# Another order for the steps of an attention and mixer kernel, from the first token mixing on

## The chip, the core and the metric

The kernel runs on one core of a Trainium2 chip. The metric is device time in microseconds (us): the median of the runs. The engines are TensorE (PE; its weight loads are listed as PEld), VectorE (DVE), ScalarE (ACT), GpSimd (POOL) and SyncE (SP, which here only starts DMAs).

## The reference

Two stages, all in float32. The first is delta-rule attention over 4 batches, 8 heads, 768 positions and 48 columns a head; the second mixes tokens at rank 32 and then channels.

```python
k_n = k / (norm(k) + 1e-06)
for t in range(S):                                   # S = 768
    y[:, :, t] = einsum('bhd,bhde->bhe', q[:, :, t], state)
    v_old = einsum('bhde,bhd->bhe', state, k_n[:, :, t])
    state = state + beta[t] * outer(k_n[:, :, t], v[:, :, t] - v_old)

x = y with its heads side by side                    # (4, 768, 384)
u = x + (x.transpose(0, 2, 1) @ U @ V).transpose(0, 2, 1)    # U 768x32, V 32x768
out = u + maximum(u @ w_ch1, 0) @ w_ch2              # 384 -> 1536 -> 384
```

## The kernel before, in words

**The attention.** The 768 positions of a batch are cut into 12 chunks of 64, and a batch into two units of 6 chunks: units n0 to n7 for batches b0 to b3. For each unit, `grams` turns k and q (`turn`, PE at L672, or for n3 on `turn_blocks`, transposes on DVE at L747) and multiplies them (`products`, L700; i0 is k with k, i1 is k with q; their results leave by ACT at L720 or DVE at L731). A triangular system per chunk is then inverted: `blocks` (L771) does so for blocks of 32 on DVE, one pair of instructions (prod at L803, xt at L809) per column, after a transpose (gs, L794) and before another (zz, L816); `joins` (L838), once for each half h0 and h1 of a unit, joins the blocks by small matmuls of 32*32 (L860 and L874 for n2 alone, with an ACT copy at L865 and a DVE step at L878 between them; then L900 and L903, an ACT copy at L908, then L918 and L921); `diagonals` (L933) puts the blocks in place by four ACT copies (L939) and two POOL memsets (L946). `prepare` (L1014; matmuls L1023 and L1034) applies the inverse to k and v. `recur` (L955) walks a batch's 12 chunks one after another, by matmuls of 16 small pieces at L1072 and L1100 with DVE steps between (z at L1085, s at L1111); `outputs` (L975; L983 and L997) forms a chunk's result, and ACT at L967 puts it into X.

**The mixer.** A batch has three groups of 256 positions, i0 to i2. `front` (L1381) multiplies X by U once a batch (L1393, with a DVE copy tt), by V for each group (L1412), adds on DVE, and turns the sum (L1436) into ut by an ACT copy (L1439). `wide` (L1449) holds the channel mixing of a group: `channels` e0 to e5 (L1465; two steps each of 6 matmuls at L1497), each followed by `relu` on ACT (L1462); `add_up` on DVE (L1524); `narrow` e0 to e3 (L1574; seven steps in a group, each 12 matmuls of L1617 in the trace), each step followed by `gather` on DVE (L1537), which adds into X and lets the result be stored. The second product of the mixing is written with seven products in place of eight, which needs the sums S1 and S2 and the weight sums. The last batch takes its first product by seven products too: `quick` (L1283), six times (f0 to f5), with matmuls at L1296, ACT copies and a final relu.

**Weights.** `load_weights` (L1147) brings fp32 weights in as pieces (`start`, SP's DMAs), which ACT (`raised`, L1198) and DVE (L1211, L1219, L1226) put into the form that PE multiplies.

**What sets the order.** Each of these functions is a generator: it yields `op(engine, cost, ...)` (L101) ahead of every step it issues and `need(...)` (L114) where it depends on a key that another announces by `emitted` (L117). `ORDER` (L144 to L350) is a table from the step's place, 0 to 2258, to the name of the generator that makes its next step there. `run()` (L381) goes through the table and advances that generator, so the instructions of every engine, and the DMAs of the SP and POOL queues, are issued in the order of the table; each engine works its own queue in order, and waits on semaphores where data or a buffer is missing. The costs in `op` play no part in what is issued. `free["pair"]` holds the four pairs of PSUM banks: a step with `take="pair"` gets the one that came free first by the table's order, and a step with `give` puts it back; `reserve` (L1442) takes pair 3 out for the mixer (its two banks are "mix"). `QUADRANTS` (L351) is empty, so full matmuls keep the form 128*128 ("F" in the code); the steps of `products`, `prepare`, `recur`, `outputs` and L1412 use 64*64 or the like ("Q"), `joins` 32*32 ("J"), L1393 128*32 ("T").

Of the kernel before, what the change touches and what calls it, by code (L numbers as in the profile page):

```python
# [27 lines left out]
def kernel(  # L28
# [116 lines left out]
    add_up b0 i0 f00: 573 585 613; add_up b0 i0 f03: 645 676 690; add_up b0 i1 f00: 795 797 800; add_up b0 i1 f03:  # L145
    818 819 824; add_up b0 i2 f00: 942 944 1042; add_up b0 i2 f03: 1023 1051 1071; add_up b1 i0 f00: 1161 1166 1186;
    add_up b1 i0 f03: 1189 1190 1191; add_up b1 i1 f00: 1309 1337 1363; add_up b1 i1 f03: 1357 1359 1368; add_up b1
    i2 f00: 1488 1493 1571; add_up b1 i2 f03: 1564 1572 1576; add_up b2 i0 f00: 1695 1717 1737; add_up b2 i0 f03:
    1728 1729 1730; add_up b2 i1 f00: 1888 1895 1906; add_up b2 i1 f03: 1886 1889 1901; add_up b2 i2 f00: 1992 2000
    2026; add_up b2 i2 f03: 2046 2047 2049; add_up b3 i0 f00: 2185 2186 2188; add_up b3 i0 f03: 2191 2192 2195;  # L150
    add_up b3 i1 f00: 2201 2202 2207; add_up b3 i1 f03: 2208 2209 2210; add_up b3 i2 f00: 2227 2228 2236; add_up b3
    i2 f03: 2224 2225 2229; blocks n0: 61 73 75 76 82 84 86 88 89 91 93 94 96 97 103 110 114 122; blocks n1: 143 157
    160 163 173 175 179 192 201 206 208 212 213 215 218 219 226 229; blocks n2: 479 496 501 502 508 512 513 514 515
    516 518 519 525 532 534 536 539 542; blocks n3: 704 720 721 729 730 733 739 741 761 765 769 771 772 773 778 779
    780 781 783 785 786 787 791 798 801 802 813 815 823 828 829 834 836 838; blocks n4: 971 982 985 987 989 996 1007
    1009 1012 1036 1038 1039 1040 1064 1074 1077 1082 1083 1087 1090 1107 1116 1119 1120 1122 1127 1129 1131 1132
    1133 1137 1138 1139 1140; blocks n5: 1168 1195 1198 1207 1218 1225 1227 1230 1231 1236 1241 1244 1249 1259 1269
    1271 1276 1278 1281 1286 1288 1291 1293 1294 1298 1311 1313 1314 1316 1323 1324 1332 1333 1351; blocks n6: 1510
    1523 1532 1541 1547 1558 1563 1566 1567 1568 1569 1596 1603 1612 1616 1617 1620 1622 1624 1645 1649 1653 1660
    1663 1665 1666 1671 1672 1673 1674 1675 1681 1684 1699; blocks n7: 1713 1724 1725 1739 1741 1744 1757 1762 1767  # L160
    1773 1775 1780 1782 1783 1800 1806 1807 1810 1817 1824 1829 1834 1837 1838 1849 1850 1856 1857 1860 1865 1866
    1867 1879 1881; both f0: 2149; both f1: 2105; both f2: 2147; both f3: 2123; both f4: 2111; both f5: 2184;
    channels b0 i0 e0: 546 547; channels b0 i0 e1: 549 550; channels b0 i0 e2: 552 553; channels b0 i0 e3: 567 574;
    channels b0 i0 e4: 588 591; channels b0 i0 e5: 604 633; channels b0 i1 e0: 768 776; channels b0 i1 e1: 777 788;
    channels b0 i1 e2: 790 792; channels b0 i1 e3: 799 803; channels b0 i1 e4: 806 807; channels b0 i1 e5: 808 814;
    channels b0 i2 e0: 898 899; channels b0 i2 e1: 907 912; channels b0 i2 e2: 935 936; channels b0 i2 e3: 950 959;
    channels b0 i2 e4: 965 969; channels b0 i2 e5: 995 1005; channels b1 i0 e0: 1118 1130; channels b1 i0 e1: 1136
    1148; channels b1 i0 e2: 1150 1151; channels b1 i0 e3: 1153 1155; channels b1 i0 e4: 1156 1158; channels b1 i0
    e5: 1159 1175; channels b1 i1 e0: 1297 1299; channels b1 i1 e1: 1300 1302; channels b1 i1 e2: 1304 1305; channels
    b1 i1 e3: 1306 1307; channels b1 i1 e4: 1326 1327; channels b1 i1 e5: 1342 1343; channels b1 i2 e0: 1430 1431;  # L170
    channels b1 i2 e1: 1432 1449; channels b1 i2 e2: 1450 1469; channels b1 i2 e3: 1470 1497; channels b1 i2 e4: 1498
    1501; channels b1 i2 e5: 1516 1530; channels b2 i0 e0: 1650 1654; channels b2 i0 e1: 1656 1669; channels b2 i0
    e2: 1686 1687; channels b2 i0 e3: 1689 1692; channels b2 i0 e4: 1697 1698; channels b2 i0 e5: 1700 1701; channels
    b2 i1 e0: 1808 1812; channels b2 i1 e1: 1813 1831; channels b2 i1 e2: 1833 1841; channels b2 i1 e3: 1843 1869;
    channels b2 i1 e4: 1871 1873; channels b2 i1 e5: 1874 1876; channels b2 i2 e0: 1950 1959; channels b2 i2 e1: 1960
    1961; channels b2 i2 e2: 1973 1979; channels b2 i2 e3: 1987 1999; channels b2 i2 e4: 2011 2027; channels b2 i2
    e5: 2033 2037; copies f0: 2127 2136; copies f1: 2082 2095; copies f2: 2129 2142; copies f3: 2086 2107; copies f4:
    2085 2103; copies f5: 2166 2168; cut f0 k0 to0: 2173; cut f0 k0 to1: 2169; cut f0 k1 to1: 2152; cut f1 k0 to0:
    2139; cut f1 k0 to1: 2106; cut f1 k1 to1: 2112; cut f2 k0 to0: 2153; cut f2 k0 to1: 2158; cut f2 k1 to1: 2163;
    cut f3 k0 to0: 2146; cut f3 k0 to1: 2154; cut f3 k1 to1: 2206; cut f4 k0 to0: 2171; cut f4 k0 to1: 2137; cut f4  # L180
    k1 to1: 2165; cut f5 k0 to0: 2181; cut f5 k0 to1: 2187; cut f5 k1 to1: 2194; diagonals n0 h0: 188 190 191 195 210
    222; diagonals n0 h1: 167 169 171 176 181 186; diagonals n1 h0: 312 315 319 336 343 353; diagonals n1 h1: 290 292
    303 338 349 358; diagonals n2 h0: 576 577 578 579 595 600; diagonals n2 h1: 632 646 665 670 705 707; diagonals n3
    h0: 854 855 860 865 870 873; diagonals n3 h1: 848 849 885 905 960 966; diagonals n4 h0: 1160 1162 1172 1197 1200
    1215; diagonals n4 h1: 1164 1192 1205 1211 1223 1226; diagonals n5 h0: 1356 1361 1365 1375 1402 1413; diagonals
    n5 h1: 1354 1380 1392 1419 1443 1444; diagonals n6 h0: 1708 1710 1711 1738 1745 1749; diagonals n6 h1: 1712 1723
    1726 1747 1753 1754; diagonals n7 h0: 1899 1905 1913 1931 1942 1945; diagonals n7 h1: 1892 1898 1911 1912 1918
    1957; first f0: 2160; first f1: 2097; first f2: 2135; first f3: 2138; first f4: 2092; first f5: 2180; front b0
    i0: 495 500 506 509 524 537; front b0 i1: 556 562 602 624; front b0 i2: 634 640 672 680; front b1 i0: 1055 1065
    1066 1078 1091 1111; front b1 i1: 1216 1224 1232 1237; front b1 i2: 1338 1348 1412 1425; front b2 i0: 1595 1599  # L190
    1605 1608 1623 1628; front b2 i1: 1633 1661 1702 1764; front b2 i2: 1801 1811 1835 1845; front b3 i0: 2041 2042
    2048 2050 2052 2054; front b3 i1: 2055 2061 2062 2067; front b3 i2: 2068 2070 2074 2076; gather b0 i0 h0 c0
    finalFalse: 671; gather b0 i0 h0 c0 finalTrue: 695; gather b0 i0 h0 c1 finalTrue: 756 1010; gather b0 i0 h1 c0
    finalFalse: 710; gather b0 i0 h1 c0 finalTrue: 757 805; gather b0 i0 h1 c1 finalFalse: 715; gather b0 i0 h1 c1
    finalTrue: 738; gather b0 i1 h0 c0 finalFalse: 820; gather b0 i1 h0 c0 finalTrue: 831; gather b0 i1 h0 c1
    finalTrue: 896 1061; gather b0 i1 h1 c0 finalFalse: 851; gather b0 i1 h1 c0 finalTrue: 881 1367; gather b0 i1 h1
    c1 finalFalse: 868; gather b0 i1 h1 c1 finalTrue: 867; gather b0 i2 h0 c0 finalFalse: 1017; gather b0 i2 h0 c0
    finalTrue: 1041; gather b0 i2 h0 c1 finalTrue: 1105 1185; gather b0 i2 h1 c0 finalFalse: 1079; gather b0 i2 h1 c0
    finalTrue: 1097 1163; gather b0 i2 h1 c1 finalFalse: 1084; gather b0 i2 h1 c1 finalTrue: 1086; gather b1 i0 h0 c0
    finalFalse: 1188; gather b1 i0 h0 c0 finalTrue: 1204; gather b1 i0 h0 c1 finalTrue: 1272 1778; gather b1 i0 h1 c0  # L200
    finalFalse: 1229; gather b1 i0 h1 c0 finalTrue: 1277 1591; gather b1 i0 h1 c1 finalFalse: 1238; gather b1 i0 h1
    c1 finalTrue: 1247; gather b1 i1 h0 c0 finalFalse: 1358; gather b1 i1 h0 c0 finalTrue: 1378; gather b1 i1 h0 c1
# [1080 lines left out]
    def quick(f):  # L1283
# [77 lines left out]
        mm(px, w1_of(f + HF, 1), t4)  # L1361
        mm(px, w1_of(f + HF, 2), t5, stop=True)
        emitted(("quick", f))
        yield op("act", act(384), rush=True)
        nc.scalar.activation(c(1, 0), px, ACTF.Relu)
        emitted(("cut", 1, 0, f), 0.06)
        yield need(("out", f))
# [328 lines left out]
```

## Time and profile before

| what | value |
|---|---|
| time, median of 3 runs | 599.98 us |
| the three runs | 596.76, 601.71, 599.98 us |
| profiled execution, span from first to last instruction | 594.9 us |
| profiled execution, own time | not given; the median stands 5.1 us above the span |
| mean granted TensorE clock | 0.943 |
| instructions in the trace | 23426 |
| DMA, read and written in HBM | 29.98 MB and 4.72 MB |
| PE, costliest lines | L1497 150.1 us (x648); L1617 w_sb,hs 96.7 us (x540) |
| DVE, costliest lines | L809 64.6 us, L803 63.3 us (x200 each) |
| ACT, costliest lines | L939 32.4 us (x64), L1462 32.2 us (x54) |

How to read it: the share of an engine's busy time is over the whole span; a matmul's end is modelled, so the start of the next step is the surer mark. "Idle before" is time in which an engine stood still just ahead of an instruction, followed by the releaser, the work that ended last ahead of it. The chain follows what released what, back from the last instruction. Position 500 of the table lies at about 110.6 us: the L1393 step of `front b0 i0`, at position 495, begins at 108.55.

### The profile page before, as it was taken

Reading aid. Unit: us, or ns where it says so; the run is one execution under the profiler, and the core shown is the slowest. Engines: PE = TensorE matmul, PEld = TensorE weight load, DVE = VectorE, ACT = ScalarE, POOL = GpSimd, SP = SyncE. Lnnn points to the kernel's source line nnn. Section 1 sums busy time; section 2 is a strip of 40 time slices with the busy share of each in tenths; the row PEclk is TensorE's granted clock in tenths of the full one; section 3 lists DMA queues with packets and bytes.
Section 4 is the critical chain, followed back from the end, with each engine's and each line's share of the span. In section 5 each row is a group of like instructions: output and inputs, shape, how many; then the busy total and the mean of one; then the engine's idle time right before and its main releaser. Section 6 shows DMA issues by size and latency. Waiting matters only on the chain.

```text
span 594.9 us, 23426 instructions
## 1 busy us (share of the span) xinstructions
PE 559.7 (94%) x10428; PEld 481.6 (81%) x10428; DVE 409.3 (69%) x1011; ACT 216.8 (36%) x442; POOL 133.3 (22%) x229
## 2 busy tenths in 40 slices
PE   3778978899999999999999999999999999999997
PEld 3578977678988887989889887889899868656997
DVE  3888758899999458999884279998883235313542
ACT  1846475446322542035224341252243321335000
POOL 8122036116010724141205214520310000000000
PEclk9855556999999999999999999999999999999999
DMA  9981639714030415240402144420401000000000
GB/s 140 180 176 24 214 80 197 152 56 79 3 65 12 68 31 92 46 91 13 82 2 43 18 83 90 79 56 2 95 7 43 4 2 4 16 8 1 26 28 28
DMA packets 89445, 36.23 MB, mean 61 GB/s; under 512 B 75456, under 2 KB 87104, under 8 KB 89344
## 3 DMA queue, kind: packets, MB, share of 16 engines
q1 hardware_dynamic: 80800, 24.69, 20.7%
q0 software_dynamic: 6944, 9.74, 8.3%
q8 instruction: 82, 1.34, 1.0%
q10 hardware_dynamic: 1600, 0.30, 0.3%
q14 instruction: 19, 0.16, 0.1%
HBM read 29.98 MB, written 4.72 MB: 58 GB/s over the span
## 4 chain that ended last, share of the span: by engine, by line
PE 83%; DVE 11%; issue 2%; ACT 2%; DMA 1%; SPq 0%; DVEq 0%; ACTq 0%
PE P L1617 27%; PE P L1497 22%; PE P L1296 7%; PE P L700 4%; DVE xt L809 3%; DVE prod L803 3%; PE P L1072 2%; PE P L860 2%; PE P L874 2%; PE P L1023 2%; PE P L1034 2%; PE P L983 2%; PE P L997 2%; PE P L1100 2%; PE P L1412 2%
## 5 line engine op out<-in xcount | busy, mean ns | idle before, releaser
L1497 PE MATMUL P<-ut,w_sb 128*128 128x256 f32 x648 | 150.1, 385 | 1.5 <-ACT ut L1439 0.9
L1497 PEld LDWEIGHTS P<-ut,w_sb 128*128 128x128 f32 x648 | 119.9, 190 | 18.7 <-ACT ut L1439 1.1
L1617 PE MATMUL P<-w_sb,hs 128*128 128x192 f32 x540 | 96.7, 331 | 0.1
L1617 PEld LDWEIGHTS P<-w_sb,hs 128*128 128x128 f32 x540 | 87.2, 190 | 3.7 <-issue 1.2
L809 DVE TENSOR_TENSOR xt<-xt,prod 128x112 f32<-128x112 f32 (+21 forms) x200 | 64.6, 323 | 6.9
L803 DVE TENSOR_TENSOR prod<-gs,xt 128x112 f32<-128x112 f32 (+21 forms) x200 | 63.3, 316 | 3.5
L1537 DVE TENSOR_TENSOR X<-X,P 128x192 f32<-128x192 f32 x84 | 29.1, 349 | 49.8 <-PE P L1617 49.4
L1462 ACT ACTIVATE hs<-P 128x512 f32<-128x512 f32 x54 | 32.2, 598 | 77.5 <-PE P L1497 65.6
L967 ACT COPY X<-P 64x192 f32<-64x192 f32 x96 | 30.0, 313 | 66.3 <-PE P L997 63.4
L1617 PE MATMUL P<-w_sb,S 128*128 128x192 f32 x288 | 50.7, 330 | 0.0
L1617 PEld LDWEIGHTS P<-w_sb,S 128*128 128x128 f32 x288 | 46.6, 190 | 2.8 <-issue 1.8
L555 POOL DMA_DIRECT2D slot<-in_v_dram x32 | 21.1, 664 | 92.3 <-DVE prod L803 60.3
L1085 DVE TENSOR_TENSOR z<-slot,P 128x192 f32<-128x192 f32 x44 | 15.5, 352 | 30.8 <-PE P L1072 29.7
L541 POOL DMA_DIRECT2D slot<-in_q_dram x40 | 24.6, 621 | 46.9 <-DVE slot L747 33.3
L939 ACT COPY slot<-zz 32x384 f32<-32x384 f32 x64 | 32.4, 509 | 7.0 <-DVE zz L878 3.9
L700 PE MATMUL P<-slot 48*64 48x64 f32 x1536 | 30.9, 231 | 2.1 <-issue 1.4
L1296 PE MATMUL P<-slot,w_sb 128*128 128x384 f32 x96 | 32.9, 486 | 0.0
L700 PEld LDWEIGHTS P<-slot 48*64 48x64 f32 x1536 | 27.9, 144 | 5.6 <-issue 2.7
L946 POOL MEMSET slot<- 32x384 f32 x32 | 13.3, 421 | 84.2 <-PE P L903 63.4
L1617 PE MATMUL P<-w_sb,slot 128*128 128x192 f32 x180 | 30.4, 327 | 0.9 <-DVE X L1537 0.9
L555 POOL DMA_DIRECT2D slot<-in_k_dram x44 | 29.4, 670 | 8.3 <-PE P L1100 7.6
L1617 PEld LDWEIGHTS P<-w_sb,slot 128*128 128x128 f32 x180 | 29.3, 190 | 1.7 <-DVE X L1537 1.5
(153 smaller groups left out, 901.4 us busy)
## 6 DMA issues: line engine op xcount, KB each, us to landing
out_dram<-X SPq DMA_DIRECT2D x22, 192.0 KB, 2.7
w_sb<-in_moe_w_ch_dram SPq DMA_DIRECT2D x10, 384.0 KB, 5.6
slot<-in_k_dram SPq DMA_DIRECT2D x48, 72.0 KB, 3.9
slot<-in_k_dram POOLq DMA_DIRECT2D x44, 72.0 KB, 3.8
slot<-in_v_dram SPq DMA_DIRECT2D x32, 72.0 KB, 3.7
slot<-in_v_dram POOLq DMA_DIRECT2D x32, 72.0 KB, 3.5
X<-in_moe_w_ch_dram SPq DMA_DIRECT2D x6, 384.0 KB, 6.1
wide<-in_moe_w_ch_dram SPq DMA_DIRECT2D x6, 384.0 KB, 5.0
```

Source lines behind the costliest of these rows:

```text
L541: queue.dma_start(out=blocked(n)[quarter(y % 4), j, g, :, 0:w], in_=src[b, 4 * g + 2 * j + par, hf * UC * L : (hf + 1) * UC * L, BK * low ...
L555: queue.dma_start(out=t[half(1 - g if name == "z" else g), :, to, 0:D], in_=src[b, 4 * g + s, hf * UC * L : (hf + 1) * UC * L, :].rearrang ...
L700: nc.tensor.matmul(p_g[half(g ^ (par * i)), par, c], kq[rows, c, j, 0, half(g)], kq[rows, c, j, i, half(g)], start=True, stop=True,)
L803: nc.vector.tensor_tensor(out=prod, in0=gb[:, :, j : j + 1, j + 1 :].to_broadcast([128, split, m, w]), in1=xb[:, :, 0:m, j : j + 1].to_bro ...
L809: nc.vector.tensor_tensor(out=xb[:, :, 0:m, j + 1 :], in0=xb[:, :, 0:m, j + 1 :], in1=prod, op=ALU.subtract,)
L939: nc.scalar.copy(pg[quarter(i), :, at, :, a : a + BK], cut(zc, h)[quarter(i)].rearrange("p r (c j) t -> p r c j t", j=2),)
L967: nc.scalar.copy(x[half(c % 2), c // 2, 4 * D * g : 4 * D * (g + 1)].rearrange("p (j r d) -> p r j d", r=2, d=D), states(p_y)[half(g)],)
L1296: nc.tensor.matmul(to, w, t, start=start, stop=stop, skip_group_check=True)
L1462: nc.scalar.activation(hs[:, fs[0] : fs[1] + 1 : fs[1] - fs[0]], p_f, ACTF.Relu)
L1497: nc.tensor.matmul(p_f[:, x], w(x, t), ut[:, t], start=(t == 0), stop=(t == KT - 1))
L1537: nc.vector.tensor_tensor(out=to, in0=to, in1=p, op=ALU.add)
L1617: nc.tensor.matmul(to, of[0], of[1], start=of[2], stop=of[3], skip_group_check=True)
```

## The change

It has two parts. The table's places 0 to 499 stay as they are; from 500 on the same steps (each name as often as before, 2,259 in all) stand in another order. Some of the entries, the places of a name's steps:

```diff
-    front b0 i0: 495 500 506 509 524 537;
+    front b0 i0: 495 505 508 514 521 524;
-    products n2 i1 j0: 517 528 538;
+    products n2 i1 j0: 500 526 544;
...
-    relu b1 i0 fs(10, 11): 1178;
+    relu b1 i0 fs(10, 11): 1210;
-    narrow b1 i0 e0: 1177 1183;
+    narrow b1 i0 e0: 1211 1213;
-    diagonals n4 h0: 1160 1162 1172 1197 1200 1215;
+    diagonals n4 h0: 1178 1191 1197 1200 1205 1206;
...
-    joins n5 h0: 1352 1382 1395 1398 1404 1409 1418 1426;
+    joins n5 h0: 1358 1371 1372 1388 1389 1391 1419 1424;
-    joins n5 h1: 1353 1388 1390 1396 1406 1411 1420 1438;
+    joins n5 h1: 1354 1374 1380 1390 1393 1394 1396 1427;
...
-    front b2 i2: 1801 1811 1835 1845;
+    front b2 i2: 1780 1789 1931 1932;
-    channels b2 i1 e0: 1808 1812;
+    channels b2 i1 e0: 1803 1805;
```

In `quick`, the wait for ("out", f), announced once DVE has added the quick step's second result, stands ahead of the last relu instead of behind it, and the relu gives the pair of banks back:

```diff
         mm(px, w1_of(f + HF, 2), t5, stop=True)
         emitted(("quick", f))
-        yield op("act", act(384), rush=True)
+        yield need(("out", f))
+        yield op("act", act(384), rush=True, give=[("pair", x)])
         nc.scalar.activation(c(1, 0), px, ACTF.Relu)
         emitted(("cut", 1, 0, f), 0.06)
-        yield need(("out", f))
-        free["pair"][x] = state["now"] + 0.06
```

As `run()` issues by the table, a `need` gives no instruction of its own; what the edit alters in what is issued is from when on the pair of banks can be handed out again.

## The prediction

> **What bounds the kernel now.** I read the page's busy shares first, then the span in stretches of 50 us, then the chain of waits that ends last, and last TensorE's timeline and its list of waits. The shares and slices:
>
> ```profile
> PE 559.7 (94%) x10428; PEld 481.6 (81%) x10428; DVE 409.3 (69%) x1011; ACT 216.8 (36%) x442; POOL 133.3 (22%) x229
> ...
> PE   3778978899999999999999999999999999999997
> PEld 3578977678988887989889887889899868656997
> DVE  3888758899999458999884279998883235313542
> ```
>
> TensorE (PE) is busy 94% of the span; slices are 14.9 us each, and from the eighth on (about 110 us, where the orders begin to differ) its digits are 8, 9 and 9 throughout. The windows (columns: PE, PEld, DVE, ACT, POOL busy, PE's clock, DMA share, GB/s) give this in us:
>
> ```profile
> 100.00:150.00 50.00, 46.08 (x1234) 37.58 (x1233) 46.35 (x98) 26.71 (x49) 18.30 (x30) 0.97 0.50 100
> 150.00:200.00 50.00, 49.88 (x879) 45.37 (x870) 44.94 (x117) 14.54 (x32) 7.58 (x13) 1.00 0.17 33
> ...
> 250.00:300.00 50.00, 49.92 (x883) 44.73 (x882) 45.95 (x119) 18.48 (x36) 15.36 (x25) 1.00 0.29 58
> ...
> 350.00:400.00 50.00, 49.74 (x750) 41.99 (x748) 47.29 (x126) 15.84 (x34) 19.09 (x32) 1.00 0.34 66
> ```
>
> Two things are to be seen. Behind 150 us PE lacks at most 1.05 us in any 50, so an order can win little there by filling idle time. And VectorE (DVE), at 45 to 47 of 50, is a second queue nearly as full: a step put in a wrong place on it delays PE at once. Idle time of PE, of the kind that an order makes, stands in the timeline (brackets: idle before, and what ended it):
>
> ```profile
> 111.98 0.88 PE L1412 MATMUL P<-tt,v_sb 64*64 64x384 f32 x8 [0.48 <-DVE prod L803]
> ...
> 115.95 8.04 PE L1497 MATMUL P<-ut,w_sb 128*128 128x256 f32 x36 [0.89 <-ACT ut L1439]
> ...
> 126.14 0.99 PE L874 MATMUL P<-zz 32*32 32x16 f32 x96 [0.43 <-ACT zz L865]
> ```
>
> Pieces of the chain (start, us, what) show a second cost that an order sets:
>
> ```profile
> 252.29 15.74 PE P L1497 x72
> ...
> 311.92 1.95 PE P L1617 x12
> 314.71 2.15 PE P L1617 x12
> ...
> 354.42 1.49 PE P L1497 x6
> ...
> 506.88 42.57 PE P L1296 x132
> 549.45 13.66 PE P L1617 x84
> ```
>
> Six matmuls of L1497 take 15.74 / 12 = 1.31 us among their like, and 1.49 where matmuls of a small form (64*64 or 32*32) come next; twelve of L1617 take 1.95 and 2.15. So leaving the full form costs 0.18 to 0.20 us, and an order with fewer such changes is shorter with no wait gone. The last two lines show the tail: the quick steps of batch 3 run back to back.
>
> **The change, part by part.** No instruction is added or removed, on any engine or DMA queue: every step name has the same count, and the 2,259 steps keep their work. Positions 0 to 499 are the same. So the sum is: changes of form, plus waits that go, plus waits that come. It is made against the profiled execution, span 594.9 us. The page gives no time of its own for that execution; the median of the three runs (599.98) is 5.1 us above its span, and I add every difference to 599.98.
>
> *Changes of form.* I counted PE's steps in both tables from position 500: 149 changes of form before, 138 after. Eleven fewer by the 0.18 to 0.20 above is −2.0 to −2.2. Pricing instead each of PE's steps by the median that its like has in the trace, ahead of the same next form, the steps sum to 466.8 us before and 464.4 after; I take −2.4. (From there to PE's last step the trace has 479.1 us, so 12.3 us are waits now.)
>
> *Waits that go.* 0.29 ahead of the L1617 step at 194.10 (behind a DVE gather), 0.24 ahead of the L700 step at 345.66, and 0.64 at 418.67, where channels follow the front whose ACT copy they need: in the new table other steps stand between in all three places. Sum −1.2. Three stay: the ends of the recurrences of batches 1, 2 and 3 (2.0, 1.0 and 1.1 us, where each small step needs the DVE result of the last) keep nearly the same neighbours, and so do the tail's two waits of 0.6 behind the gathers.
>
> *First stretch, 110 to 144 us.* Now 3.4 us of waits. In the new table two `products n2 i1` steps stand inside the front, so PE has work under the ACT copy ut (0.80 us, L1439) that it now waits 0.89 for. Against this the DVE copy of tt goes behind two more pairs of `blocks` (0.37 + 0.44 us), so the L1412 matmuls come 0.4 to 0.7 later; `load_weights 32` (0.98 us on DVE) goes ahead of `joins n2 h0`; and the bank for `prepare n2 h0` comes free behind another DVE step. Adding DVE's durations in the new order, PE step by PE step, the largest lateness is 2.3 us against 1.7 now. I take +0.7. Bounds: all 3.4 filled (−3.4), and the sum without overlap of DVE's neighbouring instructions (+3.3).
>
> *260 to 280 us (unit n4).* `relu b1 i0` for fs (10, 11) on ACT goes behind six copies of diagonals and joins (about 0.5 us each, L939 0.51), so the second half of `narrow b1 i0 e0` waits 0.7 to 0.9; nothing on PE is there to fill it, since the queue is in order. DVE has up to 2.0 us more ahead of `joins n4`, of which the matmuls in front cover most. I take +1.4; bounds 0 and +2.9.
>
> *Joins of n4, n5 and n6.* Both halves' L900/L903 steps and then the L918/L921 steps are packed with no L1617 or L1497 step between. L903 must pass through an ACT copy (L908, 0.32 us), so L918 can start 0.86 to 1.0 after it, and the other half gives 0.63 of cover: 0.25 to 0.38 a pair, more for n6, where an ACT copy of 0.51 stands ahead. In the trace such waits exist already (PE's L918 on ACT zz L908: 1.5 us in two times). With n4's counted above, I take +0.9 for n5 and n6; bounds 0 (DVE late anyway, so the wait is counted once) and +2.4.
>
> *POOL and SP.* Loads and memsets move past each other on both queues. The loads with the least lead in the new table (n3 k ahead of `prepare n3 h0`, n2 v behind a memset, n4 q, n7 q) are issued early enough by 1 to 5 us at the landing times of 3.5 to 3.9 us and 0.62 to 0.67 per issue; at nothing, as long as the memsets (0.42 each) don't wait long. What it costs if that cover is gone is a rival.
>
> *The quick steps.* The relu (L1365, 0.49 us, 6 times) is now ready only when `out` is, and gives the pair back itself. In a fixed order this only moves where the bank is handed out and which ACT or DVE work stands ahead of it. Following six quick steps (42.57 / 6 = 7.1 us each) with their banks, I find 0.2 to 0.5 us of slack at each, and one later gather in front of a `narrow b3` step: +0.25. Bounds 0 and, without the slack, 6 × 0.3 = +1.8.
>
> The sum: −2.4 − 1.2 + 0.7 + 1.4 + 0.9 + 0.25 = −0.35, so 599.6 us. With all lower ends −2.4 − 1.2 − 3.4 = −7.0 (593.0); with all upper ends −2.2 − 1.2 + 3.3 + 2.9 + 2.4 + 1.8 = +7.0 (607.0).
>
> **The rivals.** *Faster: the waits that I add are covered.* DVE's queue has been read too pessimistically; the early waits are filled and L918 finds its copies done. For it: PE's digits of 9 while DVE stands at 46 of 50 say that the present order hides such links well, and the new one fills the 0.89 and 0.64. Against it: in n5 and n6 the fillers between L903 and L918 are really gone. It gives −7.0: 593.0 us.
>
> *Slower: DVE becomes the bound.* In the three full stretches (100 to 150, 250 to 300, 350 to 400) DVE has 3.7, 4.1 and 2.7 us to spare. If the new order puts its `blocks` work ahead of PE's needs by about 3.3 us in each, as the sum without overlap says of the first, PE idles 9.9 − 3.6 = +6.3: 606.3 us. It decides from about 3.2 us a stretch. For it: the `recur b1` links are spread among DVE's `blocks n3`, and each waits for its turn there. Against it: PE then falls behind too, and the next links find DVE done, so the lateness doesn't add up over the stretches.
>
> *Slower: a load comes late.* If one of the memsets on POOL waits for an ACT copy, the loads queued behind it start that much later. One load late by its landing time costs up to 3.9 us, two 7.8: +7.5 with the rest of the sum, 607.4. For it: the POOL rows of these loads stand idle behind DVE and PE. Against it: POOL is at most 19.1 of 50 busy.
>
> *Slower: the clock drops.* The granted clock is 1.00 from 150 us on, with small forms among the full ones; the longest stretch of small forms on PE is 3.6 us now and 2.9 in the new table, so rows of this case give no reason for a drop. If it dropped to one half for one such stretch of 3 us, it would cost 3 us. The Trainium skill (TensorE: Matmul & The Clock Gate, "What's actually happening") says that the clock is halved after an idle window of about 3.4 us; the trace has a clock of 0.57 in 50 to 100 us with PE 43.4 of 50 busy, so here idle time alone doesn't explain it, and no wait that I add is near that length.
>
> **How the numbers follow.** A measurement of this kernel can tell about 1% (6.0 us) from no change: its three runs span 596.76 to 601.71. My forecast, no change beyond that, has 0.60, and its own range is 595 to 605. The waits covered: 0.17. DVE the bound: 0.16. A late load 0.06, the clock 0.01. So faster by over 1% is 0.17, within 1% 0.60, slower 0.23. The range for 8 in 10 goes to both ends of the sum: 593 to 607.
>
> **What would show it.** In the new profile PE's wait for ACT ut (0.89) should be gone and its waits on DVE between 110 and 144 us somewhat longer; L918's waits on ACT zz L908 should come in more than two places and sum to about 2.5 us instead of 1.5; L1617 should wait for ACT hs once, near 270 us, for 0.7 to 0.9; and the waits at 194, 345 and 418 us should be gone. The steps of L1497 that take 1.49 should be fewer. PE's busy sum over 500 to 550 us should stay 50.0. I am wrong if PE's busy windows behind 150 us fall below 48 of 50 (DVE or a load is the bound), if a DMA stands among the releasers of PE behind 110 us, if the clock row shows less than 1.00 there, or if the windows of 100 to 150 gain more than 3 us.

## The result: slower, by instructions that reach TensorE too late

The changed kernel takes 605.5 us (median of 6 runs, 604.97 to 608.1), the kernel before 599.87 (6 runs, 595.49 to 602.75); the ratio is 1.012, with a 95% interval of 1.0084 to 1.0157. The forecast was 599.6 and, as the likeliest case, no change beyond 1%. The profiled execution has a span of 603.3 us and an own time of 605.32, against a span of 594.9. The two spans differ by 8.4 us and the medians by 5.6: the runs of before spread over 7 us, and its profiled one was a quick one. From the first L1393 matmul (L1401 now) to PE's last matmul the two profiles have 482.95 and 492.60 us: 9.65 us were lost in the reordered part (the first 108 us took 1.25 less this time). Line numbers behind the table are 9 higher now, 8 behind `quick`.

The page of the changed kernel, the lines that answer to those of before, with the clock:

```profile
PE 564.4 (94%) x10428; PEld 486.8 (81%) x10428; DVE 408.4 (68%) x1011; ACT 216.6 (36%) x442; POOL 133.2 (22%) x229
...
PE   3888887899999999989999899989999999999997
PEld 3777876688989887979889787979889878655997
DVE  3889758999997369997695289988873144323452
...
PEclk9656557999999999999999899999999999999999
```

PE's busy time rose by 4.7 us with the same 10428 matmuls, its digits have 8s in the middle of the span that were 9s, and one slice of the clock behind 110 us is 8. The windows (columns as in the prediction: PE, PEld, DVE, ACT, POOL busy, PE's clock, DMA share, GB/s) say where:

```profile
100.00:150.00 50.00, 46.85 (x1291) 38.13 (x1290) 47.24 (x101) 26.38 (x48) 15.77 (x27) 0.99 0.46 95
150.00:200.00 50.00, 49.77 (x848) 45.05 (x848) 44.65 (x117) 14.19 (x31) 11.65 (x21) 1.00 0.21 41
...
250.00:300.00 50.00, 48.32 (x921) 43.34 (x914) 40.37 (x106) 18.16 (x35) 12.07 (x20) 0.97 0.28 55
300.00:350.00 50.00, 47.89 (x979) 41.92 (x978) 29.19 (x73) 19.79 (x40) 15.90 (x27) 0.97 0.26 49
350.00:400.00 50.00, 49.52 (x656) 42.32 (x654) 45.59 (x118) 11.59 (x26) 12.35 (x20) 1.00 0.28 56
400.00:450.00 50.00, 47.86 (x938) 42.75 (x940) 40.21 (x106) 18.88 (x40) 11.65 (x21) 0.97 0.15 37
```

Up to 250 us PE is as busy as before. Then three windows (250, 300 and 400 us) lack 1.7 to 2.1 us of PE, and the same three have a clock of 0.97. DVE, at 40, 29 and 40 of 50 there, isn't full. The timeline of PE shows the waits (in brackets the idle time before, and its releaser; the first row answers to the prediction's row of L1412):

```profile
111.61 0.88 PE L1420 MATMUL P<-tt,v_sb 64*64 64x384 f32 x8 [1.31 <-DVE tt L1407]
...
113.64 0.87 PE L1444 MATMUL P<-ident,X 128*128 128x128 f32 x6 [0.34 <-DVE X L1425]
...
266.94 0.18 PE L927 MATMUL P<-zz 32*32 32x32 f32 x1 [1.67 <-issue]
...
340.00 1.25 PE L709 MATMUL P<-slot 48*64 48x64 f32 x44 [1.86 <-issue]
...
405.14 0.26 PE L930 MATMUL P<-zz 32*32 32x32 f32 x1 [1.74 <-issue]
...
427.31 2.86 PE L1505 MATMUL P<-ut,w_sb 128*128 128x256 f32 x12 [0.40 <-issue]
```

The long waits from 266.94 us on have no engine behind them: "issue" means that the engine waited for nothing that the profile shows as a releaser. Behind those at 266.94, 340.00 and 405.14 us the clock was halved. The windows of 2 us around the first of them:

```profile
263.00:265.00 2.00, 2.00 (x137) 1.54 (x136) 2.00 (x5) 1.28 (x4) 0.85 (x3) 1.00 0.21 49
265.00:267.00 2.00, 0.33 (x37) 0.23 (x27) 2.00 (x4) 1.41 (x4) 1.89 (x5) 1.00 0.00 0
267.00:269.00 2.00, 2.00 (x57) 1.77 (x57) 1.97 (x5) 0.99 (x2) 0.37 (x1) 0.90 0.33 80
269.00:271.00 2.00, 2.00 (x7) 1.55 (x6) 1.83 (x5) 1.41 (x3) 0.00 (x0) 0.50 0.02 2
271.00:273.00 2.00, 2.00 (x9) 1.69 (x8) 0.90 (x5) 1.95 (x5) 0.00 (x0) 0.75 0.00 0
```

PE counts as busy from 267 on, but works off only 7 and 9 matmuls in 2 us. Clocks of 0.90, 0.50 and 0.75 in three windows of 2 us are 0.4 + 2.0 + 1.0 = 3.4 us at half clock. From 268.9 to 272 us one L1505 matmul lasts 606 ns in the mean, against 379 ns from 255 to 263 us:

```profile
L1505 PE MATMUL P<-ut,w_sb 128*128 128x256 f32 x9 | 3.8, 606 | 0.0
```

**What the waits have in common.** The page lists queues that carry instructions alone. The larger one:

```profile
q8 instruction: 81, 1.33, 0.9%
```

These are 81 transfers of 16 KB. PE has 20,940 instructions in the trace (20,856 matmuls and weight loads, the rest semaphores and drains), 258 to a transfer. So I numbered these in order of time and set the start of each q8 transfer beside them. A wait is taken here from the start of the last PE instruction ahead of it to the start of the first one behind it, and so is some 0.2 us longer than the idle time in brackets (0.07 and 0.48 at the two with number 17089):

| kernel | wait of PE, us | ends at | number of the first one behind it | last q8 transfer began | lag, us |
|---|---|---|---|---|---|
| before | 0.73 | 130.93 | 5825 | 128.57 | 2.36 |
| before | 0.64 | 418.67 | 17089 | 416.07 | 2.60 |
| after | 1.86 | 266.94 | 11457 | 264.49 | 2.44 |
| after | 2.08 | 340.00 | 14273 | 337.41 | 2.58 |
| after | 1.93 | 405.13 | 16321 | 402.78 | 2.35 |
| after | 0.88 | 427.31 | 17089 | 424.61 | 2.70 |

The numbers differ by whole multiples of 256: 11457 − 5825 = 22 × 256, 14273 − 11457 = 11 × 256, 16321 − 14273 = 8 × 256, 17089 − 16321 = 3 × 256. So the waits share a place in the count: I read 256 instructions as a block that one transfer brings, and call its first instruction a border. Each wait ends at a border, 2.35 to 2.70 us behind the start of a transfer. That transfer began when PE was already in the block before, 0.28 to 2.93 us behind its first instruction; of all 62 behind 105 us in the new order, 32 began 0.6 to 1.2 us behind that instruction and 14 ahead of it. A block of full-form matmuls takes some 20 us (12 of L1617, with their weight loads 24 instructions, take 1.95), and the next one is there in time. In the joins, the 256 instructions from 263.70 us on (with those of L909, L912, L927 and L930) had all begun 1.38 us later, long before the 3.2 us that the next block took to come.

### The profile page after: what moved, and what is told of

It is laid out like the page before. It is cut to its first block, busy times and chain, and to the rows that moved or that the text cites. A ratio compares the mean times of both kernels' runs of the same rounds, so it can differ in the third digit from the quotient of the medians.

```text
span 603.3 us, 23426 instructions
## 1 busy us (share of the span) xinstructions
PE 564.4 (94%) x10428; PEld 486.8 (81%) x10428; DVE 408.4 (68%) x1011; ACT 216.6 (36%) x442; POOL 133.2 (22%) x229
## 4 chain that ended last, share of the span: by engine, by line
PE 85%; DVE 8%; issue 3%; ACT 1%; DMA 1%; SPq 0%; DVEq 0%; ACTq 0%
PE P L1625 28%; PE P L1505 25%; PE P L1305 7%; PE P L709 3%; PE P L1081 2%; PE P L992 2%; PE P L883 2%; PE P L1006 2%; PE P L1109 2%; PE P L1032 2%; PE P L1043 2%; PE P L869 2%; PE P L1420 1%; PE P L1444 1%; DVE xt L818 1%
## 5 line engine op out<-in xcount | busy, mean ns | idle before, releaser
L1505 PE MATMUL P<-ut,w_sb 128*128 128x256 f32 x648 | 153.9, 390 | 0.4 <-issue 0.4
L1505 PEld LDWEIGHTS P<-ut,w_sb 128*128 128x128 f32 x648 | 121.3, 192 | 18.2 <-issue 0.7
L1625 PE MATMUL P<-w_sb,hs 128*128 128x192 f32 x540 | 97.0, 333 | 0.0
L1625 PEld LDWEIGHTS P<-w_sb,hs 128*128 128x128 f32 x540 | 88.7, 192 | 3.8 <-issue 2.1
L1625 PE MATMUL P<-w_sb,S 128*128 128x192 f32 x288 | 49.5, 327 | 0.0
L1625 PEld LDWEIGHTS P<-w_sb,S 128*128 128x128 f32 x288 | 46.9, 190 | 1.3 <-DVE X L1545 0.6
L550 POOL DMA_DIRECT2D slot<-in_k_dram x40 | 24.5, 620 | 69.2 <-DVE z L1094 26.8
L1120 DVE TENSOR_TENSOR s<-s,P 128x192 f32<-128x192 f32 x40 | 14.0, 349 | 31.7 <-PE P L1109 28.2
L709 PE MATMUL P<-slot 48*64 48x64 f32 x1536 | 32.2, 235 | 2.6 <-issue 1.9
L564 POOL DMA_DIRECT2D slot<-in_k_dram x44 | 29.6, 675 | 7.9 <-PE P L1109 7.7
```

What stands on the lines that cost most here:

```text
L550: queue.dma_start(out=blocked(n)[quarter(y % 4), j, g, :, 0:w], in_=src[b, 4 * g + 2 * j + par, hf * UC * L : (hf + 1) * UC * L, BK * low ...
L564: queue.dma_start(out=t[half(1 - g if name == "z" else g), :, to, 0:D], in_=src[b, 4 * g + s, hf * UC * L : (hf + 1) * UC * L, :].rearrang ...
L709: nc.tensor.matmul(p_g[half(g ^ (par * i)), par, c], kq[rows, c, j, 0, half(g)], kq[rows, c, j, i, half(g)], start=True, stop=True,)
L1505: nc.tensor.matmul(p_f[:, x], w(x, t), ut[:, t], start=(t == 0), stop=(t == KT - 1))
L1625: nc.tensor.matmul(to, of[0], of[1], start=of[2], stop=of[3], skip_group_check=True)
```

## The experiments

**Theory 1** is this supply: what decides is which instructions are borders, and the clock falls after the wait. **Theory 2** is the prediction's: DVE, ACT or a bank is late at those steps. The two can be told apart by a change that moves the borders and nothing else. Small matmuls into a bank that is overwritten later, put ahead of everything, do this; PE waits there for its first load anyway (up to 9.1 us). Each is four PE instructions, two matmuls and two weight loads in the trace.

```diff
     make_identity(nc, ident)
+    for _ in range(11):
+        nc.tensor.matmul(
+            P[0:32, 7, 0:16], ident[0:32, 0:32], ident[0:32, 0:16], start=True, stop=True
+        )
```

**a44**, the new order with 44 instructions of padding.

> The new order, with 11 small matmuls (44 PE instructions, results never read) put ahead of everything, while PE waits 9 us for its first load. No other instruction moves. Theory 1 (PE's instructions arrive in blocks of 256, and a block that is reached less than about 2.4 us behind the start of its transfer holds PE up): all block borders shift by 44 instructions, so the waits of 1.86, 2.08, 1.93 and 0.88 us at 266.9, 340.0, 405.1 and 427.3 us go, and so do the three stretches of half clock; time 593 to 596, against 605.5. Theory 2 (the waits come from DVE or ACT being late, or from a bank not being free): the same waits stand at the same steps, 605 to 606.

Measured: 592.95 us, ratio to the old order 0.9908 (0.9872 to 0.9944), 12.5 us below the new order unpadded (605.5, from the first comparison). The four waits are gone:

```profile
263.00:265.00 2.00, 2.00 (x146) 1.58 (x145) 2.00 (x4) 1.55 (x5) 0.87 (x3) 1.00 0.17 45
265.00:267.00 2.00, 2.00 (x75) 1.83 (x65) 2.00 (x4) 1.99 (x6) 1.89 (x5) 1.00 0.03 8
267.00:269.00 2.00, 2.00 (x11) 1.75 (x10) 1.97 (x4) 1.93 (x5) 0.27 (x1) 1.00 0.28 74
269.00:271.00 2.00, 2.00 (x13) 1.92 (x12) 1.83 (x5) 1.95 (x5) 0.00 (x0) 1.00 0.00 0
```

These are the same steps as in the windows above: PE is busy throughout, with DVE as full as before, and the clock is 1.00 (it is so from about 104 us to the end). Theory 2 falls: DVE and ACT have the same instructions in the same order. **a44r**, the same file once more in five rounds:

> The new order with 44 PE instructions of padding once more, for a closer ratio: 592 to 594, 0.8 to 1.1% below the old order.

594.74 us, ratio 0.9925 (0.9896 to 0.9954): a little above what was expected, and again below both kernels.

**a192**, the same with 48 matmuls.

> The new order with 48 small matmuls (192 PE instructions) ahead. Theory 1: the borders fall once more into dense stretches of small matmuls, a little off the present ones: waits of 1.6 to 1.8 us in the joins of n4 (near 267), n5 (near 319) and n6 (near 405), with half clock behind them, none at 340 and 427, and one of 1.1 near 126; time 603 to 606. Theory 2: 605 to 606, with the wait at 340 still there and none of 1.8 at 319.

Measured: 610.81 us, ratio 1.0209 (1.0152 to 1.0266), 5 above the range. The waits stand at 273.3 (1.93), 326.5 (1.69) and 410.5 us (1.98), in the joins of n4, n5 and n6 as expected; half clock came behind the first and the last only. Not expected were 1.63 at 347.1, 1.95 at 132.1 in place of 1.1 near 126, and a first L1393 matmul (L1401 of the new order) at 111.74 instead of 107.30. All five waits end on a first instruction of a block, 2.25 to 2.76 us behind a transfer's start.

**a256**, a whole block of padding, as a control.

> The new order with 64 small matmuls, 256 PE instructions, one whole block, ahead of everything. Control for the padding itself. Theory 1: the borders of the blocks fall on the same instructions as without padding, so the waits near 267, 340, 405 and 427 us come back, at the same matmuls and within 0.4 us of their lengths, with half clock behind the first three: 604 to 607. If it was the padding (a warmer array, a later start) that made the run with 44 fast: 593 to 596.

Measured: 605.75 us. The first three waits came back, 2.02, 2.02 and 1.78 us, each with half clock; the fourth with 0.50. From the first L1393 matmul on it takes 492.82 us, the new order unpadded 492.60. So it isn't the padding, but its place in the count of 256.

**a120**, 30 matmuls, a place that theory 1 called harmless.

> The new order with 30 small matmuls, 120 PE instructions. A second place of the borders that theory 1, reckoned from the trace of the new order, calls harmless: one wait of 1.1 us near 126 us, none above 0.5 behind it and no half clock; from the first L1393 matmul to PE's last 482 to 483.5 us (481.2 with 44, 492.6 without), time 593 to 596. Theory 2: 605 to 606.

A miss: 607.36 us. From 152 us to PE's last matmul no wait is above 0.8, and the clock is 1.00. But 8.7 us are lost ahead of the first L1393 matmul (115.98 against 107.30), where the trace has border waits too, the longest 4.1 us at 20 us; I had reckoned from 108 us on only. The wait expected near 126 came at 136.0 with 1.51, one of 1.89 at 151.1 was not expected, and half clock stood around 116 and 137. The stretch behind the first L1393 takes 485.97, not 482 to 483.5.

**b48**, the old order with 12 matmuls.

> The old order with 12 small matmuls (48 PE instructions) ahead. Theory 1: a border falls into the joins of n2, a wait of about 2.0 us near 132 and perhaps 1.5 us more by a half clock behind it, while the wait of 0.64 at 418.7 goes: 601 to 603 against 599.9. Theory 2: no change, 599 to 601.

The wait came at 132.1 us (1.81, on a border) with half clock behind it, the one at 418.7 went, and the stretch from the first L1393 took 485.42 us, 2.5 more than unpadded. The time did not follow: 598.27, ratio 1.0005 (0.9971 to 1.004), where theory 1 had 601 to 603. The old order's own runs spread over 7 us in that comparison, and what the other executions lost is not in a profile; this stays open.

**bq**, the old order with the edit in `quick` alone (the second diff of the change).

> The old order with the edit in quick alone. Theory 1 and theory 2 both put the loss elsewhere: no change, 599 to 601, and the tail from the first L1296 matmul on as long as before (82.8 us). The rival that the relu's later place or the bank's later return costs up to 0.3 us a quick step: 601 to 602.

599.75 us, ratio 0.9999 (0.9964 to 1.0034); 483.09 us from the first L1393, against 482.95. The edit costs nothing that these runs can tell.

**an4**: one step of the new order moved up among the joins of n4.

```diff
     ORDER = {int(y): name for name, at in ORDER for y in at.split()}
+    moved = ORDER[1189]
+    for y in range(1189, 1160, -1):
+        ORDER[y] = ORDER[y - 1]
+    ORDER[1160] = moved
```

> The new order with one step moved: the second step of channels b1 i0 e4 (six L1505 matmuls, 1.30 us, 12 PE instructions) goes from place 1189, behind the joins of n4, to place 1160, among them. All other borders stay where they are. Theory 1: the block that ends in those joins takes 1.3 us longer to be worked off, so the wait of 1.86 us falls to about 0.55, too short for the clock to fall (1.7 us more): 602 to 603 against 605.5. Theory 2 (the wait is for ACT's or DVE's result): ACT and DVE get 1.3 us more too and the wait falls alike, but the wait's end is then no longer tied to a block border; without the clock's part 604.

Measured: 601.68 us, ratio 1.0057 (1.0014 to 1.01). With the added lines L930 has become L934, and L1625 L1629:

```profile
268.35 0.18 PE L934 MATMUL P<-zz 32*32 32x32 f32 x1 [0.53 <-issue]
...
274.88 2.22 PE L1629 MATMUL P<-w_sb,hs 128*128 128x192 f32 x12 [1.07 <-ACT hs L1474]
```

The border's wait fell from 1.67 to 0.53 in brackets, or from 1.86 to 0.72 by the table's measure, where 0.55 was reckoned, and the clock stayed at 1.00 there. So one full-form step of 1.3 us in a dense stretch took 1.14 us of wait and a stretch of half clock away. The second line is the wait for relu that the prediction had put at 0.7 to 0.9: with the border's wait ahead of it, it had been hidden. Not all of the 3.8 us below the new order is due to the moved step: in this profile the clock also stayed up behind the wait at 339.6 us (2.31).

**a6q**: why did the transfer for the block at 340.0 begin 2.93 us behind the border before, and not 0.6 to 1.2? Sixteen loads land just then.

```diff
                     yield op(e, 0.65, port=False)
-                    queue.dma_start(
+                    if (name, n) != ("q", 6):
+                        queue.dma_start(
```

> The new order without the sixteen loads of q for unit n6 (48 and 24 KB each, on the SP and POOL queues, landing between 331 and 338 us); n6 then works on what the buffer held, so half a batch is computed from other numbers, with as many instructions on PE. PE's block that starts with the matmul at 340.0 us had its transfer begun only 2.93 us behind the block before it, where most begin within 0.6 to 1.2. Theory 1a (the transfer of the instructions stood behind these loads): it begins within 1.3 us of the border before, the wait of 2.08 us falls to 0.5 or less, the half clock behind it goes: 601 to 603 against 605.5. Theory 1b (the late start comes from PE's own queue): wait and time unchanged, 605 to 606.

n6 works on old numbers here, so the run serves the timing alone. Measured: 600.63 us, a little less than expected. The windows from 330 to 345 us, first of the new order, then without the loads:

```profile
330.00:335.00 5.00, 5.00 (x169) 4.50 (x171) 2.32 (x7) 1.38 (x2) 3.39 (x6) 1.00 0.47 80
335.00:340.00 5.00, 3.14 (x109) 2.51 (x102) 0.68 (x3) 1.34 (x2) 3.45 (x6) 1.00 0.90 189
340.00:345.00 5.00, 5.00 (x88) 4.48 (x88) 1.21 (x4) 2.47 (x5) 0.00 (x0) 0.66 0.10 18
```

```profile
330.00:335.00 5.00, 5.00 (x117) 4.52 (x115) 2.03 (x5) 1.38 (x2) 0.00 (x0) 1.00 0.00 0
335.00:340.00 5.00, 5.00 (x231) 4.49 (x230) 0.97 (x3) 1.63 (x3) 0.00 (x0) 1.00 0.02 7
340.00:345.00 5.00, 5.00 (x138) 4.28 (x131) 1.87 (x7) 2.83 (x6) 0.00 (x0) 1.00 0.27 42
```

With the DMA engines at 0.90, PE lacks 1.86 us and then runs at 0.66; with them at 0.02, the transfer begins 0.68 us behind the border (336.06), no wait is left and the clock stays 1.00. That is theory 1a: the transfer of the instructions stood behind the loads. Five loads of k and two stores, which the new order has between 331 and 338.5 us as well, moved out of that time too, so it is the traffic as a whole that this shows, not the sixteen loads alone.

**w2 and w5**: does any wait bring the half clock? Both pad by 40 and make PE wait for ACT in the midst of full-form matmuls, two copies (w2) or five (w5, shown) long.

```diff
                 p_f = mixed(m).rearrange("p (x n) -> p x n", x=2)
+                if (b, i, e) == (1, 0, 2):
+                    nc.tensor.matmul(
+                        p_f[0:32, 0, 0:16], ident[0:32, 0:32], ident[0:32, 0:16], start=True, stop=True
+                    )
+                    for _ in range(5):
+                        nc.scalar.copy(p_f[:, 1], p_f[:, 0])
```

> The new order with 40 PE instructions of padding, and one wait for data made on purpose in the middle of the long run of L1505 matmuls near 255 us: ahead of channels b1 i0 e2 a small matmul, two ACT copies of 256 columns inside the bank that channels is about to overwrite, and the real matmuls wait for them. It tells whether any wait of PE brings the half clock, and from what length. Expected: a wait of 1.0 to 1.3 us, no half clock, time 0.8 to 1.5 above the run with 44: 593.7 to 594.5.

> As the last, with five ACT copies in place of two. Expected, if an idle stretch of some 1.8 us is enough for the clock whatever PE waits for: a wait of 2.0 to 2.5 us, then one stretch of 3.4 us at half clock, which costs 1.7: 596.5 to 597.5. If only a wait for instructions brings the half clock: 595 to 595.5.

Measured: 595.2 us (ratio 0.995, 0.9914 to 0.9986) and 597.88 (1.0003, 0.9967 to 1.0039). w2 waits 1.01 us as expected. Its time is above the range, which was reckoned from a44's 592.95, and 0.5 above a44r's 594.74. From the first L1401 matmul on, its profile has 482.37 us against a44's 481.20. w5, timeline and windows:

```profile
258.16 0.23 PE L1506 MATMUL P<-ident 32*32 32x16 f32 x2
260.38 0.92 PE L1515 MATMUL P<-ut,w_sb 128*128 128x256 f32 x3 [2.00 <-ACT P L1510]
```

```profile
258.00:262.00 4.00, 2.00 (x13) 1.57 (x10) 3.73 (x10) 3.45 (x8) 0.00 (x0) 1.00 0.23 41
262.00:266.00 4.00, 4.00 (x20) 3.53 (x19) 3.68 (x9) 1.13 (x4) 1.58 (x2) 1.00 0.10 25
```

A wait of 2.18 us (from the last matmul's start to the next), and the clock stays at 1.00. What was expected from the length alone is wrong in this execution: from the first L1401 matmul on it has 483.18 us, 1.98 more than a44, about the wait alone. The median lies above the case without half clock, which the profile doesn't explain. Over all profiles, 12 of 16 border waits of 1.7 to 2.5 us behind 105 us were followed by 3.4 us of half clock, and so were two shorter ones of a120 (1.62 and 1.51). These lie among small matmuls. Where a wait lies in time counts as well: within each trace, the times at which the clock changes differ by whole multiples of 3.41 us. Two of the four waits without half clock, an4's 2.31 and a192's 1.95, are divided by a point of this grid (0.93 + 1.38 and 0.66 + 1.29 us), while the twelve with half clock have 1.59 to 2.35 us between two points, and the clock falls at the second. The other two (1.59 of a120's 1.89 at 151.1 us, w2's 1.77 at 110.5 us) and w5 (1.88) kept the clock with as much. That the activity around the wait counts too fits a120 and w5, which have full-form matmuls behind the wait, but that isn't shown; it stays open.

## Why the prediction was wrong

**The step that failed** is a term that the sum did not have: PE's supply of instructions. The prediction's sum was "changes of form, plus waits that go, plus waits that come", with another engine's result, a bank or a load behind each wait, and it priced PE's steps by rows that hold as long as instructions are there. The half clock behind such waits had no place in it either. That 605.5 lies inside the range of 593 to 607 is luck: the range was made of other terms. The signs were in the profile of before:

```profile
130.93 0.21 PE L903 MATMUL P<-zz,slot 32*32 32x32 f32 x1 [0.54 <-issue]
...
418.67 1.67 PE L1497 MATMUL P<-ut,w_sb 128*128 128x256 f32 x7 [0.57 <-issue]
```

Both waits have "issue" as releaser. I put the first into the sum of the first stretch and the second down to "the front whose ACT copy they need"; its instruction is number 17089, a border, and in the new order the wait is there again, at the same number and another place.

What this term measures, each step's time less the median of its like: waits at borders in the new order 1.85 + 2.39 + 2.03 + 0.77, and 0.33 + 0.26 + 0.26 + 0.28 at four smaller ones, 8.2 us; in the old order 0.70 + 0.44 + 0.64 = 1.8. Half clock: 0.42 + 1.26, 0.42 + 0.86 and 0.18 + 1.38, 4.5 us in the steps behind three waits. 8.2 − 1.8 + 4.5 = 10.9. Without it the new order would gain: a44 has 481.20 us from the first L1393 to the last matmul, the old order 482.95, the new one 492.60. The difference of 11.4 to a44 agrees with this term within 0.5. Set side by side matmul by matmul (7,962 in each, in the same steps), the new order is 0.44 us behind a44 at 265 us, 3.21 at 285, 3.91 at 335, 7.61 from 350 to 400, 11.11 at 415 and 11.40 at the end: nearly all is lost around three borders.

**The other terms**, read in a44, where the border waits of that size are gone. *Changes of form*, −2.4: this is the difference of the steps' stall-free sums. The waits are what the time has beyond such a sum (12.9 us in a44, 12.3 before), so it can't be tested apart from them; together they give the 1.75 that a44 is shorter. The price of 0.18 to 0.20 a change was read on leaving the full form, and of the eleven changes fewer only seven are that (72 before, 65 after, by the traces). *Waits that go*, −1.2: those at 194 and 345 us went; the third was a border. *First stretch*, +0.7: the wait for ut went, the one for tt grew from 0.48 to 1.29 (0.8 more, not 0.4 to 0.7), and the waits up to 142 us sum to 2.4 against 3.4: −1.0. *n4*, +1.4: 0.59 for relu and 0.17 in the joins. *n5 and n6*, +0.9: 0.22 each. The two waits on which this was based (L918 on ACT zz L908, 1.5 us) stand at 47.2 and 49.7 us, ahead of the reordered part, and the new order's list has no more of them. *Quick*, +0.25: bq's 0.14 is no difference that can be measured. The sum of −0.35 was thus pessimistic by 1.4 us; the waits that it added came in smaller than it had them.

**The rivals.** DVE as the bound (0.16, 606.3 us) came near in time and is wrong: padding on PE's queue alone takes the waits away, with DVE's order unchanged. A load that comes late (0.06) looked at DMA traffic but not at what it delays: no wait of PE behind 110 us has a DMA as releaser, and at 340 us it was the transfer of instructions that came late. The clock (0.01) was priced at 3 us and cost 4.5, behind waits of about 2 us that I hadn't foreseen; what the prediction said of it, that no added wait is near the length, stood on the missing term. The trace agrees with the Trainium skill (TensorE: Matmul & The Clock Gate, "What's actually happening") on the half clock and its stretches of 3.4 us, not on a whole idle window as its condition: a wait of 1.86 us was enough. The Trainium skill also has blocks of 256 instructions on a queue of the engine's own (Runtime: NRT & Kernel Launch, "Instruction fetch mechanics"), which the table above bears out. That the cost of a border is "mostly hidden", as it says there, holds here for blocks of full-form matmuls, and fails by up to 2.1 us in the changed kernel, where 256 instructions are worked off faster than the next ones come.

The marks that the prediction set were right ones: PE below 48 of 50 (47.89 and 47.86), a clock below 1.00 (0.97). What it read into the first, that DVE or a load would be the bound, was not.

## What to carry to other kernels

Where an engine waits and "issue" is named, number its instructions and look at the instruction queue's transfers: if the first ones behind the waits are whole numbers of blocks apart, the engine is short not of data but of instructions. Dense runs of tiny matmuls need longer ones between them, or a border that falls elsewhere. In a static program a few dummy instructions move it, but they have to be tried: 44 made the new order faster, 120 and 256 left its time about as it was (607.36 and 605.75 us), and 192 made it slower (610.81). Every later edit moves the borders again, and bulk loads at the wrong moment can delay the block (a6q).

## What was not expected of the hardware

- PE's instructions come in blocks of 256; the first of a block ran no sooner than 2.25 us behind the start of its transfer, in all waits above.
- With the DMA engines at 0.90 such a transfer began 2.93 us behind the border before, with them at 0.02 it began 0.68 us behind it (one profile each).
- Waits of 1.78 to 2.45 us among small matmuls were followed by 3.4 us of half clock in 12 cases; 2.18 us among 128*128 matmuls wasn't, in one. The clock changes on a grid of 3.41 us, and two long waits that a point of it divided passed without.
- Eleven matmuls of no use, in a time when PE had nothing to do, made the new order 10.8 to 12.5 us faster in two runs, and left it 0.8 to 0.9% faster than the old one.
